# Five early groups instead of six, and later weights for them, in a kernel of banded attention, a low-rank mix, a channel layer and a gated layer

## The chip, the cores and the metric

One NeuronCore of a Trainium2 chip runs the whole program. The metric is the device time of one execution in microseconds (us). Engines: TensorE (PE in the rows, PEld its weight loads), VectorE (DVE), ScalarE (ACT), GpSimd (POOL) and SyncE (SP, which here only issues DMAs).

## What is computed

Four batches of 576 tokens. First comes attention with 8 heads of 64, scores limited to the 128 latest keys with a linear bias per head. Its output x (4 x 576 x 512) goes through the rest:

```
h = xt @ U @ V;  u = x + h.transpose(0, 2, 1)          # rank 32, over the tokens of a batch
y = u + np.maximum(u @ w_ch1, 0.0) @ w_ch2             # channel layer, 512 -> 2048 -> 512
h = np.maximum(y @ w_in, 0.0);  u, v = halves of h     # gated layer
out = (u * (w_spatial-mix of normalised v + b)) @ w_out
```

U, V and the weight matrices arrive as float64, so each of their words is put together on the chip from two 32-bit halves.

## The kernel before, in words

**How the order comes about.** The kernel does not write its instruction order by hand. It hands every step to a planner (`Plan`) as a task with an engine, a cost in the planner's own table, the buffers that it reads and writes, and a due number (`prio`). `Plan.run` goes through a simulated time: whenever an engine is free, it takes among the tasks whose inputs are there the one with the lowest due number. So a due number is no start time: a task with a high number still runs early where nothing else is ready, and it only steps back behind tasks with lower numbers that are ready at the same moment. DVE tasks marked `port` also wait until POOL is idle in the planner's time. The result is a fixed order on each engine, SP's queue of DMAs included, and on the chip each engine follows that order and waits where an input is late.

**Attention.** `heads(b, pair)` (L544) treats two heads of a batch at a time. The 16 pairs have due numbers p0 = 0, 20, 40, ..., 300 (10 per head; batch 0 has 0 to 60, batch 1 80 to 140). Within a pair the steps follow at p0 + 0 (loads of q and k, L553, L554), + 1 (scores on PE, L574), + 2 and + 3 (bias and row maximum on DVE, L582), + 3 and + 4 (exponentials on ACT, L587), + 4 (reciprocals of the sums, L597, L599), + 4 and + 5 (scaling of the probabilities on DVE, L607, or POOL, L605), then transposes (L614), the product with v (L628) and copies (L321 or L322). After two pairs `turned` transposes the output (L649); after four, `low_rank` (due 79 + 80 b, L665, L677, L682) adds the rank-32 mix, and the u of that batch is complete.

**Channel layer.** The 2048 hidden columns are cut into 16 blocks of 128, in four parts of 5, 4, 4 and 3 blocks (`parts`). Of part 0 there are ten weight tensors, called c = 0 to 9 here: c = 2f is the 512 x 128 piece of w_ch1 of block f, c = 2f + 1 the 128 x 512 piece of w_ch2. Each is loaded as 512 KB by one DMA (L354, due `early`), and converted (due `prio`): an absolute value on ACT (L360), a clip (L364 on POOL for c < 3, else L366 on DVE), and three DVE passes (L367, L370, L373) put the float32 together; then it is split exactly into two float32r halves, high (L383 on POOL for c < 5, else L321) and low (L388 on POOL). All DVE passes of it are `port` tasks.

Products are taken as three matmuls (high x high, low x high, high x low). `ffn_group` (L447) treats some tokens against the blocks of one part: it splits u into halves (L435, L438), multiplies with w_ch1 (L464 to L466), takes relu and the low half (L471 on ACT, L473 on DVE), multiplies with w_ch2 (L501 to L503), and adds into y (L511). It has two forms:
- early groups (`early=True`): `nb` groups of 256 tokens, part 0 alone, due 10000 + g on PE, so behind all attention work that is ready. They run between attention's matmuls. They have one buffer f1 for the first product (two blocks at a time) and one buffer acc for the second. Their evacuations have due number `evac` = 40. The split halves of u take four of the eight buffers of the ring x, so two groups are split at a time.
- late groups: 512 tokens at a time, from due 20000 on, with four buffers for the first product and four for the second. They need the pool that is opened when attention's buffers are given up, and four buffers of the ring x. Part 0 of the tokens that no early group took comes first, then parts 1, 2 and 3 of all tokens.

With `nb=6` early groups take tokens 0 to 1535, and part 0 of the other 768 is done by late groups of 512 and 256. One group of 256 tokens and part 0 has 120 matmuls (60 for each product).

The names and lines that matter:

```
part_of_hidden(0, r_wa, lambda c: 10 * (K["w0"] + K["w0s"] * c),     # L700 conversion due
                        lambda c: 10 * (K["d0"] + K["d0s"] * c), ...) # L701 load due
for g in range(NB):                                                   # L710
    ffn_group(g * 256, 256, parts_w[0], 1e4 + g, True, K["evac"], True)
t0 = NB * 256 if qi == 0 else 0                                       # L725
while t0 < NT:
    n = min(512, NT - t0)
```

V (L542) has due 40 for its conversion and 41 for its load.

Of the kernel before, what the change touches and what calls it, by code (L numbers as in the profile page):

```python
# [263 lines left out]
def tile_kernel(ctx, tc, qT, kT, v, U, V, w1, w2, w_in, wspT, bsp, w_out, bias, out):  # L264
# [32 lines left out]

    r_wa = Ring(in_left, "wa", max(12, 2 * K["parts"][0]))
    r_u = Ring(in_left, "u", 16)
    r_y = Ring(in_left, "y", 12)  # L300
    r_raw = Ring(in_left, "raw", 2)
    r_st = Ring(in_left, "st", K["nst"])
    r_h = Ring(in_left, "h", 8)
# [11 lines left out]

    PARTS = K["parts"]

# [10 lines left out]
    def engines(kind, usual):  # L328
        return BOTH if kind in K["flex"] else (usual,)

# [61 lines left out]
    def part_of_hidden(qi, ring, prio, early=lambda c: None, on_pool=lambda c: (False, False)):  # L392
        res = []
        for f in range(PARTS[qi]):
            c0 = (sum(PARTS[:qi]) + f) * 128
            two = []
            for i, args in enumerate(((block(w1, 0, E, c0, c0 + 128, 4), 4, 128), (block(w2, c0, c0 + 128, 0, E), 1, E))):
                c = 2 * f + i
                two.append(weights(ring, *args, prio(c), early(c), on_pool(c)))
            res.append(two)  # L400
        return res
# [137 lines left out]
    def low_rank_weights(prio, early, prio_v, early_v):  # L539
        single(u32, [(0, block(U, 0, 128, 0, RANK)), (1, block(U, 64, S, 0, RANK, 4))], 5, RANK, prio, None, early)  # L540
        P.add("DVE", 0.1, lambda: nc.vector.memset(u32[64:, 0], 0.0), w=[u32], prio=prio)
        single(v32, [(0, stacked(block(V, 0, RANK, 0, S), 4))], 1, S, prio_v, None, early_v)  # L542
# [143 lines left out]
    for h0 in range(0, H, 2):  # L686
        P.dma(128, 256, lambda h0=h0: nc.sync.dma_start(out=bias_t[:, h0 : h0 + 2], in_=bias[:, h0 : h0 + 2]),
              w=[bias_t.part(h0 // 2)], prio=10 * h0 + 0.5)
    low_rank_weights(15, 2, 10 * K["low"], 10 * K["lowd"])
    parts_w = [None] * 4  # L690
    for b in range(B):
# [7 lines left out]
        if b == 0:  # L699
            parts_w[0] = part_of_hidden(0, r_wa, lambda c: 10 * (K["w0"] + K["w0s"] * c),  # L700
                                        lambda c: 10 * (K["d0"] + K["d0s"] * c),  # L701
# [241 lines left out]

K = dict(parts=(5, 4, 4, 3), flex='xeht', cp=3, wp=5, low=4.0, w0=4.5, w0s=1.23, nb=6, evac=40.0, nst=3, d0=3.8, d0s=0.91, lowd=4.1)


# [38 lines left out]
```

## Time and profile before

| what | value |
|---|---|
| median of 3 runs | 805.63 us (803.71 to 806.95) |
| the profiled execution | 801.91 us, of it 800.1 us span from the first to the last instruction |
| PE busy | 767.1 us (96% of the span), 4852 matmuls |
| DVE, ACT, POOL busy | 430.7, 330.8, 278.0 us (54, 41, 35%) |
| chain that ended last | PE 84%, DVE 10%, DMA 3%, issue 1%, ACT 1% |

The chain that ended last is the work followed back from the last instruction, at each step to what released it. Busy shares are averages over stages with different limits: attention takes some 218 us of the span, the channel layer's late groups and the gated layer the rest. A matmul's duration in the rows is that of one pipelined instruction; what a matmul costs in a row of them is the distance between two starts.

### The profile page before, as it was taken

How to read it: one execution, taken by the hardware profiler on the slowest of the kernel's cores; microseconds unless marked ns; L12 is line 12 of the kernel's file. 1: busy time of each engine (PE TensorE's matmuls, PEld its weight loads, DVE VectorE, ACT ScalarE, POOL GpSimd, SP SyncE). 2: the span in 40 equal slices, each digit the busy share in tenths (PEclk: the TensorE clock that was granted, in tenths of full speed). 3: DMA queues.
4: the chain of work that ended last, by engine and by line, in shares of the span. 5: the costliest groups of instructions: out<-in, count | busy, mean ns of one | idle time of the engine just before them, and what ended most of it. 6: DMA issues, size and time to landing. Idle time of an engine off the chain costs nothing.

```text
span 800.1 us, 12918 instructions
## 1 busy us (share of the span) xinstructions
PE 767.1 (96%) x4852; PEld 654.4 (82%) x4852; DVE 430.7 (54%) x1128; ACT 330.8 (41%) x905; POOL 278.0 (35%) x354
## 2 busy tenths in 40 slices
PE   6779899999989999999999999999999999999998
PEld 4557777888888898888987889888998898898897
DVE  5789958678579367222487225832474415315220
ACT  6748848567453144121344214441343332332222
POOL 1545323120146146221376213762346114124021
PEclk9988999999999999999999999999999999999999
DMA  9842303210060052000320003000300000100101
GB/s 251 273 154 77 102 16 106 75 48 29 3 225 2 1 163 100 1 1 1 128 83 1 1 0 106 1 1 0 94 4 2 27 27 1 54 14 1 52 2 66
DMA packets 28834, 45.82 MB, mean 57 GB/s; under 512 B 4964, under 2 KB 18020, under 8 KB 28772
## 3 DMA queue, kind: packets, MB, share of 16 engines
q1 hardware_dynamic: 28772, 45.00, 17.6%
q8 instruction: 38, 0.62, 0.3%
q14 instruction: 24, 0.20, 0.1%
HBM read 40.27 MB, written 4.72 MB: 56 GB/s over the span
## 4 chain that ended last, share of the span: by engine, by line
PE 84%; DVE 10%; DMA 3%; issue 1%; ACT 1%; POOL 0%; SPq 0%; ACTq 0%; DVEq 0%; POOLq 0%
PE at L464 5%; PE at L465 5%; PE at L466 5%; PE sc L501 5%; PE sc L503 5%; PE sc L502 5%; PE at L614 3%; PE sc L574 3%; PE acc L501 3%; PE at L628 3%; PE acc L503 3%; PE f L464 3%; PE acc L502 3%; PE f L465 3%; PE f L466 3%; PE sc L769 2%
## 5 line engine op out<-in xcount | busy, mean ns | idle before, releaser
L438 POOL TENSOR_TENSOR x<-u,xc 128x192 fp32r<-128x192 f32 (+4 forms) x108 | 89.9, 865 | 136.2 <-ACT xc L435 133.4
L473 DVE SCALAR_TENSOR_TENSOR h<-at,h 128x512 fp32r<-128x512 f32 (+1 forms) x49 | 30.6, 624 | 115.5 <-ACT h L471 115.4
L471 ACT ACTIVATE h<-at 128x512 fp32r<-128x512 f32 (+1 forms) x49 | 26.7, 544 | 130.8 <-PE at L466 130.2
L587 ACT ACTIVATE p<-p,nmax 128x256 f32<-128x256 f32 (+2 forms) x160 | 72.8, 458 | 12.3 <-DVE nmax L582 11.9
L582 DVE CUSTOM_DVE_ANT_0 p<-sc,bias 128x256 f32<-128x256 f32 (+2 forms) x160 | 50.4, 362 | 17.0 <-PE sc L574 16.2
L614 PE MATMUL at<-ident,p 128*128 128x128 f32 x288 | 42.5, 288 | 13.5 <-DVE p L607 9.3
L574 PE MATMUL sc<-kr,qr 64*128 64x256 f32 (+2 forms) x320 | 43.9, 402 | 8.1 <-DMA kr<-in_kT 4.5
L388 POOL TENSOR_TENSOR wa<-st,wa 128x512 fp32r<-128x512 f32 x26 | 36.2, 1394 | 42.9 <-ACT wa L321 33.0
L614 PEld LDWEIGHTS at<-ident,p 128*128 128x128 f32 x288 | 33.2, 146 | 21.6 <-issue 6.9
L501 PE MATMUL acc<-h,wa 128*128 128x256 f32 (+1 forms) x150 | 47.5, 317 | 1.0 <-DVE y L511 0.9
L503 PE MATMUL acc<-h,wa 128*128 128x256 f32 (+1 forms) x150 | 45.0, 300 | 1.2 <-DVE h L473 1.1
L502 PE MATMUL acc<-h,wa 128*128 128x256 f32 (+1 forms) x150 | 44.6, 297 | 0.0
L466 PE MATMUL f<-x,wa 128*128 128x256 f32 (+1 forms) x148 | 44.4, 300 | 0.0
L574 PEld LDWEIGHTS sc<-kr,qr 64*128 64x128 f32 x320 | 29.9, 209 | 15.3 <-issue 6.7
L784 POOL TENSOR_TENSOR u<-y,u 128x576 fp32r<-128x576 f32 x16 | 23.0, 1456 | 54.8 <-ACT u L782 54.8
L471 ACT ACTIVATE h<-f 128x512 fp32r<-128x512 f32 (+1 forms) x34 | 18.0, 531 | 55.2 <-PE f L466 55.1
L464 PE MATMUL f<-x,wa 128*128 128x256 f32 x120 | 36.1, 300 | 4.6 <-DVE h L473 3.6
L607 DVE TENSOR_SCALAR p<-p,rinv 128x256 f32<-128x256 f32 (+2 forms) x128 | 39.7, 379 | 0.2
L503 PE MATMUL sc<-h,wb 128*128 128x512 f32 (+1 forms) x105 | 38.8, 370 | 0.0
L502 PE MATMUL sc<-h,wb 128*128 128x512 f32 (+1 forms) x105 | 38.8, 369 | 0.0
L501 PE MATMUL sc<-h,wb 128*128 128x512 f32 (+1 forms) x105 | 38.8, 369 | 0.0
L465 PE MATMUL at<-xc,wb 128*128 128x512 f32 (+1 forms) x104 | 38.5, 371 | 0.0
(329 smaller groups left out, 2347.9 us busy)
## 6 DMA issues: line engine op xcount, KB each, us to landing
wa<-in_w SPq DMA_DIRECT2D x18, 512.0 KB, 4.8
wb<-in_w SPq DMA_DIRECT2D x14, 512.0 KB, 5.5
qr<-in_qT SPq DMA_DIRECT2D x16, 288.0 KB, 4.0
kr<-in_kT SPq DMA_DIRECT2D x16, 288.0 KB, 3.5
vr<-in_v SPq DMA_DIRECT2D x16, 256.0 KB, 2.8
wa<-in_w_in SPq DMA_DIRECT2D x8, 512.0 KB, 4.4
out<-h SPq DMA_DIRECT2D x15, 256.0 KB, 2.0
wb<-in_w_out SPq DMA_DIRECT2D x4, 512.0 KB, 3.7
```

Source lines behind the costliest of these rows:

```text
L438: nc.gpsimd.tensor_tensor(out=tl[il][:, o : o + m], in0=ub[:, s : s + m], in1=f32(th[ih][:, o : o + m]), op=ALU.subtract)
L464: nc.tensor.matmul(o, wt[:, 0, k], a[ia], start=k == 0, stop=False)
L465: nc.tensor.matmul(o, wt[:, 1, k], a[ia], start=False, stop=False)
L466: nc.tensor.matmul(o, wt[:, 0, k], l[il], start=False, stop=k == 3)
L471: P.add("ACT", act(per * n), lambda f1=f1, hh=hh: nc.scalar.activation(out=hh.ap(), in_=f1.ap(), func=AF.Relu), r=[f1], w=[hh], prio=evac)
L501: nc.tensor.matmul(o, wt[:, 0, 0, c], hh[:, j], start=i == 0 and x == 0, stop=False, skip_group_check=True)
L502: nc.tensor.matmul(o, wt[:, 1, 0, c], hh[:, j], start=False, stop=False, skip_group_check=True)
L503: nc.tensor.matmul(o, wt[:, 0, 0, c], hl[:, j], start=False, stop=i == len(wts) - 1, skip_group_check=True)
L574: nc.tensor.matmul(s[j][:, c0 : c0 + n], qr[d, q0 : q0 + 128], kr[d, k0 : k0 + n], start=True, stop=True)
L582: nc.vector.tensor_tensor_reduce(out=p[:nq, c0 : c0 + nk], in0=s[:nq, c0 : c0 + nk], in1=bias_t[:nq, h, b0 : b0 + nk], scale=-0.125, scala ...
L587: nc.scalar.activation(out=p[:nq, c0 : c0 + nk], in_=p[:nq, c0 : c0 + nk], func=AF.Exp, scale=-1.0, bias=nmax[:nq, sl, t : t + 1], accum_o ...
L614: P.add("PE", 0.109, lambda pt=pt, c=c, p=pp[bk][j], c0=c0: nc.tensor.transpose(pt[:, c : c + 128], p[:, c0 : c0 + 128], ident), r=[pp[bk] ...
```

## The change

```
-K = dict(parts=(5, 4, 4, 3), flex='xeht', cp=3, wp=5, low=4.0, w0=4.5, w0s=1.23, nb=6, evac=40.0, nst=3, d0=3.8, d0s=0.91, lowd=4.1)
+K = dict(parts=(5, 4, 4, 3), flex='xeht', cp=3, wp=5, low=4.0, w0=6.5, w0s=1.23, nb=5, evac=40.0, nst=3, d0=5.5, d0s=0.91, lowd=4.1)
```

- `nb` 6 to 5: early groups take tokens 0 to 1279, and part 0 of the other 1024 is done by two late groups of 512.
- `w0` 4.5 to 6.5: the due numbers of the ten conversions go from 45, 57.3, 69.6, ..., 155.7 to 65, 77.3, 89.6, ..., 175.7, that is 20 more, the distance of two heads (one pair).
- `d0` 3.8 to 5.5: those of the ten loads go from 38, 47.1, ..., 119.9 to 55, 64.1, ..., 136.9.

The planner then makes a new order from these numbers on all engines and on SP.

## Rows read from the trace of the kernel before

**Rows 1.** Busy by stretch: PE, PEld, DVE, ACT, POOL (instructions), granted clock, DMA share, GB/s.

```profile
4.50:57.00 52.50, 40.74 (x324) 30.14 (x324) 40.68 (x152) 33.91 (x114) 20.78 (x25) 0.90 0.74 223
57.00:109.00 52.00, 45.62 (x382) 37.82 (x378) 47.47 (x170) 38.61 (x130) 22.59 (x31) 0.93 0.31 95
109.00:159.00 50.00, 48.37 (x470) 40.47 (x462) 35.91 (x151) 32.29 (x114) 10.61 (x22) 1.00 0.25 72
...
217.00:304.00 87.00, 81.95 (x557) 75.21 (x556) 57.26 (x103) 35.25 (x74) 40.25 (x40) 1.00 0.31 106
```

**Rows 2.** PE's instructions that read part 0's weights (wa), in batches 1 and 2.

```profile
57.00:109.00 52.00, 14.96 (x90) 0.93 0.31 95
109.00:159.00 50.00, 20.19 (x138) 1.00 0.25 72
```

**Rows 3.** Timeline of PE after attention: start, duration, [idle before, releaser].

```profile
229.34 0.38 PE L464 MATMUL f<-x,wa 128*128 128x256 f32 x1 [1.92 <-DVE h L473]
...
235.39 0.38 PE L464 MATMUL f<-x,wa 128*128 128x256 f32 x1 [1.48 <-DVE h L473]
...
241.60 0.36 PE L501 MATMUL acc<-h,wa 128*128 128x256 f32 x1 [0.92 <-DVE y L511]
...
245.27 0.28 PE L464 MATMUL f<-x,wa 128*128 128x256 f32 x1
...
259.19 0.39 PE L503 MATMUL acc<-h,wa 128*128 128x256 f32 x1 [0.73 <-DVE h L473]
```

**Rows 4.** Busy time in 20 us of late groups of 512.

```profile
320.00:340.00 20.00, 20.00 (x89) 16.40 (x88) 4.81 (x7) 2.82 (x7) 4.33 (x7) 1.00 0.00 1
```

**Rows 5.** Timeline of POOL after attention: splits of group 5, then the late group.

```profile
218.02 0.74 POOL L438 TENSOR_TENSOR x<-u,x 128x256 fp32r<-128x256 f32 x1 [34.98 <-PE at L677]
...
236.16 7.06 POOL L438 TENSOR_TENSOR x<-u,xc 128x192 fp32r<-128x192 f32 x8
```

**Rows 6.** Timeline of DVE in batch 0: pair 1's scaling, then around c = 0, 1.

```profile
21.81 2.53 DVE L607 TENSOR_SCALAR p<-p,rinv 128x64 f32<-128x64 f32 x10
...
39.53 0.76 DVE L367 TENSOR_SCALAR st<-st 128x512 uint32<-128x512 uint32 x2
...
41.41 1.29 DVE L373 SCALAR_TENSOR_TENSOR st<-wa,st 128x512 uint32<-128x512 uint32 x2
42.61 1.03 DVE L597 TENSOR_SCALAR rinv<-sums 128x10 f32<-128x10 f32 x1
...
43.93 5.12 DVE L607 TENSOR_SCALAR p<-p,rinv 128x64 f32<-128x64 f32 x10
```

**Rows 7.** Timeline of ACT: the last exponential of pair 3.

```profile
40.32 0.20 ACT L587 ACTIVATION_READ_ACCUMULATOR p<-p,nmax 128x1 f32 x1
```

**Rows 8.** Timeline of POOL: first and last of four splits of c = 0, 1.

```profile
42.17 1.44 POOL L383 TENSOR_TENSOR wa<-st,one 128x512 fp32r<-128x512 f32 x1 [4.64 <-DVE st L373]
...
46.03 1.42 POOL L388 TENSOR_TENSOR wa<-st,wa 128x512 fp32r<-128x512 f32 x1
```

**Rows 9.** Waits of PE, 40 to 62 us: in total, times, longest.

```profile
PE at L614 <- DVE p L607: 3.5, 2, 2.8
```

**Rows 10.** Waits of PE, 57 to 114 us.

```profile
PE at L614 <- DVE p L607: 3.1, 2, 2.1
```

**Rows 11.** Tile wa, 0 to 130 us: last DVE pass of the ten conversions, durations, first and last start.

```profile
L373 DVE SCALAR_TENSOR_TENSOR st<-wa,st x10: 678/684/925, 41.4 to 103.0; 128x512 uint32<-128x512 uint32 x10
```

**Rows 12.** Timeline of SP: the load of c = 0, then pair 2's q.

```profile
7.14 0.59 SPq L354 DMA_DIRECT2D wa<-in_w  x1
8.52 0.34 SPq L553 DMA_DIRECT2D qr<-in_qT  x1
```

**Rows 13.** Busy time and granted clock at the start of batch 1.

```profile
60.00:65.00 5.00, 3.78 (x18) 2.72 (x18) 5.00 (x23) 5.00 (x22) 5.00 (x7) 0.61 0.49 134
65.00:70.00 5.00, 5.00 (x31) 4.59 (x32) 4.93 (x19) 2.81 (x13) 2.43 (x4) 0.71 0.11 42
70.00:75.00 5.00, 4.92 (x38) 3.69 (x35) 5.00 (x19) 3.79 (x15) 0.60 (x1) 1.00 0.37 118
```

## The prediction

> **What bounds the kernel now.** I read busy time by stretch first, then the waits of PE in each stretch, then the timelines of the engines around those waits. The first view says where time can be won at all [rows 1]. In batch 0 (4.50 to 57 us) PE is busy 40.74 of 52.5 us, in batch 1 45.62 of 52, in batch 2 48.37 of 50, and from the end of attention to the end of part 0 (217 to 304 us) 81.95 of 87. So there are 11.8 + 6.4 + 1.6 + 5.05 us without a matmul, and the granted clock is 0.90 and 0.93 of full in the first two. Everything behind 304 us is late groups and the gated layer, which the change doesn't touch; it shifts as a whole. From batch 2 on PE is the bound, and a step taken off another engine gives nothing; before that DVE is the limit more often (47.47 of 52 us busy in batch 1).
>
> Early groups are what PE does between attention's matmuls: 90 matmuls' worth in batch 1, 138 in batch 2 [rows 2]. They are no extra work, only work in another place, so the sum has three kinds of terms: work that is cheaper in another form, idle time that goes, idle time that comes.
>
> **Six groups to five: the work.** Removed are one early group and the late group of 256; added is a second late group of 512. Matmuls of 256 columns start 0.12 us apart (30 from 241.60 to 245.27 us) [rows 3], so 2 x 120 of them take 28.8 us. Those of 512 columns come at 89 in 20 us, 0.225 us each [rows 4]; 120 take 27.0 us. That is 1.8 us less on PE, which is the path here. The splits, evacuations and additions into y are of the same tokens in fewer pieces; they are costed at nothing, since PE waits for them only at the places that follow.
>
> **Six groups to five: the waits.** The 5.05 us without a matmul after attention are four waits, 1.92, 1.48, 0.92 and 0.73 us [rows 3]. All are of one kind: an early group has one f1 and one acc buffer, DVE is 57 of 87 us busy with part 1's conversions besides [rows 1], and nothing else is ready for PE. The first two lie in group 4's first product, the third before its second half, the last in group 5. Why is nothing else ready? The late group's splits run on POOL from 236.16 us, while group 5's ran at 218.02 us [rows 5]: both want the four buffers of ring x that group 3 gives up, and group 5 has them. With five groups the late group gets them 18 us sooner, and PE can take its matmuls (four buffers for the first product) when group 4 waits. The last wait goes with group 5. Ends: nothing gained beyond 0.73, or all 5.05; I take 3.0, since the third wait is for y, on a DVE as busy as before, and the first comes only some 2 us after the late splits could be done.
>
> **Later weights: batch 0.** In the timeline of DVE, the three passes of c = 0 and of c = 1, six instructions, run from 39.53 to 42.61 us, ahead of pair 3's reciprocals, and those (1.03 us) ahead of pair 3's ten scalings, which take 5.12 us [rows 6]. Pair 3's last exponential had ended by 40.5 us [rows 7]. Due numbers decide here: 45 and 57.3 against 64 for the reciprocals. With 65 and 77.3 the conversions step behind. What is on the path is 42.61 - 40.5 = 2.1 us of conversion, and the slow scalings: ten took 2.53 us for pair 1 [rows 6], 2.6 us less; beside them POOL ran the four splits of c = 0 and 1 (42.17 to 47.45 us) [rows 8]. PE waited for these scalings twice, 3.5 us together [rows 9]. Ends: 0, where the planner finds another place for the same work that is as bad, and 2.1 + 2.6 = 4.7, with the stretched reciprocals 5.5. I take PE's own recorded wait, 3.5. Next in line is then the transposes' and copies' chain of pair 3 and batch 0's low-rank mix, late by their own length.
>
> **A rule on that.** The Trainium skill, SBUF — State Buffer, section Who interferes with whom, says that VectorE and GpSimd share a pair of ports under an exclusive lock, and whichever comes second blocks. By it the four splits only find other DVE instructions to block wherever they go, and the 2.6 us would be moved, not saved; the sum would be 1 to 2 us worse. The traces can't settle that, as the new neighbours aren't in them.
>
> **Later weights: SP's queue.** The load of c = 0 is issued at 7.14 us, ahead of pair 2's q at 8.52 us [rows 12]: due 38 against 40. With 55 it steps behind pair 2's loads, the third piece of the bias, V and pair 2's v; the other nine move one place or so each. 512 KB at the 223 GB/s of this stretch [rows 1] are 2.3 us by which these come sooner. No wait of PE is put down to them in the rows I read, so I take 0, with -2.3 as the other end; a loss is excluded before c = 1, whose last pass on DVE is itself 20 due later. No wait is added to SP, only order.
>
> **Later weights: batch 1.** The ten conversions end on DVE between 41.4 and 103.0 us [rows 11]. One pair of heads is about 52 / 4 = 13 us, so the last two or three land behind batch 1, in batch 2, where DVE is 35.91 of 50 us busy [rows 1] and has room. That relieves DVE at the end of batch 1, where PE waited twice for scalings, 3.1 us together [rows 10]. Against it, group 0 starts a pair later and has fewer matmuls to offer while batch 1 waits for DVE. It has 90 there now, 10.8 us at 0.12; one pair of the four later, up to half of it, 5.4 us, is displaced to where PE is full already, and is paid if batch 1 doesn't get shorter by as much. Ends -3.1 and +5.4; I take the middle, +1.
>
> **The sum.** -1.8 - 3.0 - 3.5 + 0 + 1.0 = -7.3 us. Against the profiled execution's own 801.91 us that is 794.6. That execution lies 3.7 us below the median of 805.63, and the forecast is for a median, so 805.63 - 7.3 = 798.3, say **798.5 us**.
>
> **Rivals.** A measurement of this kernel can tell about 0.5%, 4 us, from no change.
>
> First, **the conversions collide elsewhere**. A due number holds a task back only where another is ready; in the planner's time DVE may be free, and c = 0 and 1 land in an equally bad place. Then batch 0 and 1 give nothing in sum and the late group's splits, queued on POOL behind part 1's, come no sooner. For it: the order on each engine is fixed by costs that the chip doesn't keep (a third pass is planned alike for all, and took 678 to 925 ns [rows 11]). Against it: pair 3's reciprocals were ready and did lose by due number. What stays is 1.8 + 0.73: 805.63 - 2.5 = 803.1.
>
> Second, on the other side, **batch 1 is starved**. Place: PE from 57 to 75 us. At 60 to 65 and 65 to 70 us the clock is 0.61 and 0.71 of full, so mostly the lower level of 1.2 GHz, after a stretch in which PE stood waiting; at 70 it is back at 2.4 GHz [rows 13]. In between lie the first 24 matmuls of group 0, from 65.23 us. If these come a pair later, the slow stretch lasts as much longer: 3.78 x 0.39 + 5.00 x 0.29 = 2.9 us once more, beside the displaced 5.4. With the sure 2.5 off, that is +5.8: 811.4. It decides when batch 1 holds fewer than some 45 group-0 matmuls and still takes 52 us. For it: DVE is the fuller engine there. Against it: batch 0 ending sooner brings batch 1 forward, and three conversions leave it. The Trainium skill, TensorE: Matmul & The Clock Gate, section HAM oscillation — how this bites in real kernels, says that gaps in the matmuls put the engine back to half rate until it works densely again, which speaks against taking filler out of a stretch with gaps. By that rule the second rival's extra 2.9 us come; the trace agrees that the clock fell after waits.
>
> **How the numbers follow.** Forecast (faster by over 4 us) 0.58; first rival 0.27; second 0.15. The best ends of all terms together give -1.8 - 5.05 - 5.5 - 2.3 - 3.1 = -17.8, which won't meet at once; half of the way from the sum to it is -12.5, 793. To the other side the range takes in the first rival and half of the second, 808. So 791.5 to 808.
>
> **What would show it.** In the changed profile: c = 0's passes on DVE behind pair 3's scalings, and those ten near 2.5 us; batch 0 over by 54 us instead of 57; the last conversion at 108 to 120 us; after attention, the late group's splits by 230 us and at most one wait of PE over 1 us; part 0 over some 7 us sooner. I am wrong if batch 1 shows as much idle PE as before with fewer group-0 matmuls and a clock below full beyond 70 us, if the waits after attention stay near 5 us, or if what is won before 57 us is gone again by 109 us.

## The result and the profile after

The changed kernel takes 792.23 us (median of 4 runs, 788.29 to 793.14) against 804.67 us for the kernel before (4 runs beside it, 803.35 to 806.95): a ratio of 0.9833 [0.9805, 0.9861], 13.4 us less by the ratio. In a second measurement (five runs against nine of the kernel before) it was 790.39 us and 0.9817 [0.9785, 0.9848]. The forecast was 798.5 us, 7.1 less than the median then known: right in sign, but little more than half of the gain. The first measurement lies 0.7 us inside the stated range, the second 1.1 us outside it.

The profiled execution of the changed kernel took 791.57 us, with a span of 789.8. From here on the span is cut where the work itself has its marks: the first low-rank matmul of each batch (L665), which ends the batch's attention, and the last matmul of part 0. The five cuts and the rest, for the kernel before (columns as in [rows 1]):

```profile
0.00:53.94 53.94, 38.07 (x268) 28.30 (x268) 37.66 (x147) 33.19 (x112) 19.58 (x32) 0.91 0.73 221
53.94:108.62 54.68, 47.93 (x415) 39.33 (x415) 50.23 (x173) 40.83 (x135) 25.15 (x36) 0.94 0.34 102
108.62:158.70 50.08, 48.45 (x463) 40.55 (x462) 36.18 (x151) 32.29 (x114) 10.61 (x22) 1.00 0.25 72
158.70:212.65 53.95, 53.72 (x505) 45.65 (x504) 37.99 (x160) 32.01 (x117) 5.62 (x13) 1.00 0.09 29
212.65:303.74 91.09, 86.04 (x621) 78.54 (x620) 59.11 (x106) 36.11 (x76) 39.99 (x40) 1.00 0.30 101
303.74:800.00 496.26, 492.91 (x2587) 422.04 (x2585) 209.59 (x392) 156.39 (x352) 177.04 (x213) 1.00 0.08 28
```

And for the changed kernel:

```profile
0.00:49.41 49.41, 37.59 (x269) 28.55 (x269) 33.48 (x149) 32.00 (x111) 12.65 (x25) 0.93 0.74 216
49.41:104.20 54.79, 47.83 (x398) 37.56 (x397) 53.06 (x176) 39.14 (x128) 27.52 (x34) 0.91 0.40 122
104.20:156.84 52.64, 52.33 (x492) 44.28 (x492) 38.83 (x156) 32.21 (x116) 15.44 (x31) 1.00 0.24 70
156.84:209.60 52.76, 52.65 (x493) 44.62 (x492) 37.73 (x160) 32.03 (x117) 5.87 (x14) 1.00 0.10 30
209.60:295.18 85.58, 83.97 (x500) 72.03 (x500) 67.92 (x109) 36.85 (x72) 40.91 (x37) 1.00 0.33 109
295.18:789.80 494.62, 490.90 (x2586) 422.07 (x2584) 203.72 (x382) 154.56 (x349) 174.48 (x211) 1.00 0.09 28
```

The second column is the length of each cut in us. Batch 0 is 4.53 us shorter, batch 1 0.11 longer, batch 2 2.56 longer, batch 3 1.19 shorter, part 0 after attention 5.51 shorter, the rest 1.64 shorter: 10.3 us between these two executions. PE's instructions on part 0's weights number 72, 168 and 169 in batches 1 to 3, where the same cuts of the kernel before hold 90, 139 and 181: 409 against 410, so the head start at the end of attention is the same, only shifted by one batch.

The waits of PE after attention (209 to 296 us; line, what it waited for, total, times, longest), against the four of [rows 3]:

```profile
PE acc L501 <- ACT h L471: 1.2, 1, 1.2
PE acc L503 <- DVE h L473: 0.3, 1, 0.3
```

The late group's splits stand where the prediction put them: 20 us ahead of [rows 5], and 6.1 us behind the end of attention instead of 23.5 (timeline of POOL):

```profile
215.73 5.82 POOL L438 TENSOR_TENSOR x<-u,xc 128x448 fp32r<-128x448 f32 x8 [0.51 <-ACT xc L435]
```

In batch 0 the passes of c = 0 and 1 stand behind pair 3's scalings, as against [rows 6] (timeline of DVE):

```profile
42.77 2.85 DVE L607 TENSOR_SCALAR p<-p,rinv 128x64 f32<-128x64 f32 x10
45.55 0.75 DVE L367 TENSOR_SCALAR st<-st 128x512 uint32<-128x512 uint32 x2
46.22 1.28 DVE L370 SCALAR_TENSOR_TENSOR st<-wa,st 128x512 uint32<-128x512 uint32 x2
47.42 1.28 DVE L373 SCALAR_TENSOR_TENSOR st<-wa,st 128x512 uint32<-128x512 uint32 x2
```

The ten scalings take 2.85 us instead of 5.12. The splits of c = 0 and 1 on POOL have moved with the conversions: they run from 48.18 us on, beside the next weight's passes, which take 1.47 and 1.64 us where the same passes can take 0.68 (timeline of DVE):

```profile
50.01 1.47 DVE L370 SCALAR_TENSOR_TENSOR st<-wa,st 128x512 uint32<-128x512 uint32 x1
51.52 1.64 DVE L373 SCALAR_TENSOR_TENSOR st<-wa,st 128x512 uint32<-128x512 uint32 x1
```

Behind them stand the additions that complete u (L682), for which PE waits 1.1 us; in the kernel before it was 0.2, with one slow pass (1.64 us) there.

Something new is in the timeline of ACT:

```profile
23.55 0.72 ACT L360 ACTIVATE v<-raw 128x576 f32<-128x576 f32 x1 [5.65 <-DMA raw<-in_V]
```

ACT stands 5.65 us before it copies the low-rank factor V (3.21 us in the kernel before), and PE then waits 4.0 us for a copy that ACT makes behind it (3.0 us before).

In batch 1 the wait for scalings has nearly gone, and the wait for the conversions of part 0's weights has grown from 0.8 us to 3.4 (waits of PE, 49 to 105 us, against [rows 10]):

```profile
PE f L464 <- ACT wa L321: 2.0, 1, 2.0
PE f L465 <- POOL wa L388: 1.4, 1, 1.4
...
PE at L614 <- DVE p L607: 0.4, 1, 0.4
```

### The profile page after: what moved, and what is told of

Its sections match the earlier page's. It is cut to its first block, busy times and chain, and to the rows that moved or that the text cites. A ratio compares the mean times of both kernels' runs of the same rounds, so it can differ in the third digit from the quotient of the medians.

```text
span 789.8 us, 12642 instructions
## 1 busy us (share of the span) xinstructions
PE 765.3 (97%) x4732; PEld 649.1 (82%) x4732; DVE 434.7 (55%) x1129; ACT 326.8 (41%) x891; POOL 276.9 (35%) x349
## 4 chain that ended last, share of the span: by engine, by line
PE 85%; DVE 10%; DMA 2%; ACT 2%; issue 1%; POOL 0%; SPq 0%; ACTq 0%; DVEq 0%; POOLq 0%
PE at L464 5%; PE at L465 5%; PE at L466 5%; PE sc L502 5%; PE sc L501 5%; PE sc L503 5%; PE at L614 3%; PE at L628 3%; PE acc L501 3%; PE sc L574 3%; PE acc L503 3%; PE acc L502 3%; PE f L464 3%; PE sc L769 2%; PE f L465 2%; PE f L466 2%
## 5 line engine op out<-in xcount | busy, mean ns | idle before, releaser
L438 POOL TENSOR_TENSOR x<-u,xc 128x64 fp32r<-128x64 f32 (+5 forms) x108 | 91.0, 879 | 126.8 <-ACT xc L435 125.7
L574 PE MATMUL sc<-kr,qr 64*128 64x256 f32 (+2 forms) x320 | 47.0, 414 | 8.0 <-DMA kr<-in_kT 4.4
L574 PEld LDWEIGHTS sc<-kr,qr 64*128 64x128 f32 x320 | 31.9, 216 | 16.6 <-issue 6.5
L501 PE MATMUL acc<-h,wa 128*128 128x256 f32 (+1 forms) x130 | 42.1, 324 | 1.4 <-ACT h L471 1.2
L503 PE MATMUL acc<-h,wa 128*128 128x256 f32 (+1 forms) x130 | 39.8, 306 | 0.3 <-DVE h L473 0.3
L502 PE MATMUL acc<-h,wa 128*128 128x256 f32 (+1 forms) x130 | 39.5, 304 | 0.0
L466 PE MATMUL f<-x,wa 128*128 128x256 f32 (+1 forms) x128 | 38.7, 303 | 0.0
L435 ACT CAST xc<-u 128x64 fp32r<-128x64 f32 (+5 forms) x108 | 38.4, 435 | 0.5 <-PE at L677 0.5
L464 PE MATMUL at<-xc,wb 128*128 128x512 f32 (+1 forms) x104 | 38.4, 369 | 0.0
L465 PE MATMUL at<-xc,wb 128*128 128x512 f32 (+1 forms) x104 | 38.3, 369 | 0.0
```

The lines of the kernel that those rows point to most:

```text
L438: nc.gpsimd.tensor_tensor(out=tl[il][:, o : o + m], in0=ub[:, s : s + m], in1=f32(th[ih][:, o : o + m]), op=ALU.subtract)
L464: nc.tensor.matmul(o, wt[:, 0, k], a[ia], start=k == 0, stop=False)
L465: nc.tensor.matmul(o, wt[:, 1, k], a[ia], start=False, stop=False)
L466: nc.tensor.matmul(o, wt[:, 0, k], l[il], start=False, stop=k == 3)
L501: nc.tensor.matmul(o, wt[:, 0, 0, c], hh[:, j], start=i == 0 and x == 0, stop=False, skip_group_check=True)
L502: nc.tensor.matmul(o, wt[:, 1, 0, c], hh[:, j], start=False, stop=False, skip_group_check=True)
```

## The experiments

Three things had to be told apart: what each half of the change gives, where 1.6 us of the rest went in which nothing was edited, and why the runs gain more than two profiles side by side. The expectations of the first four call the terms of the prediction theory A.

**The two halves.** Five groups alone (of the dictionary K):

```diff
-nb=6
+nb=5
```

> Five early groups alone (nb=5), the weights as early as before. Theory A (the two halves of the change add up): 1.8 us less work on PE and some 3.4 us of waits after attention gone, so 5.2 us faster than before (ratio 0.9935), and in the profile at most 2 us of waits of PE between 215 us and the end of part 0. Rival B (the waits went because the later weights changed what is left after attention): only the 1.8 us of work, ratio 0.998, waits after attention still near 5 us.

Measured: 799.31 us (6 runs), 0.9922 [0.9899, 0.9945], that is 6.3 us less, where theory A had 5.2 and rival B 1.8. Part 0 after attention took 85.54 us, with 1.5 us of waits, and the rest 494.5, all as in the changed kernel: the waits go with the sixth group, and theory A holds for this half. But batch 0 ended at 56.26 us and batch 1 at 113.49, where the profile that I had worked from has 53.94 and 108.62 with the same order of work up to there. The weights alone:

```diff
-w0=4.5 d0=3.8
+w0=6.5 d0=5.5
```

> Later weights alone (w0=6.5, d0=5.5), six early groups. Theory A: batch 0 ends 4.6 us sooner as in the changed kernel, batch 1 holds fewer matmuls of group 0 and gives some 1.5 us back, the waits after attention stay near 5 us; 3 us faster in all, ratio 0.996. Rival B: the later weights also take the waits after attention away: 8 to 10 us faster, ratio 0.989.

Measured: 796.66 us, 0.9896 [0.9869, 0.9923], 8.4 us less. Batches 0 and 1 end at 50.23 and 102.50 us, and the rest takes 496.3. That is the size that rival B had, but not its way: part 0 after attention still takes 90.81 us, with 3.3 us of waits. The halves add up: 6.3 + 8.4 = 14.7, and the whole gives 13.4 to 14.7. So the five groups are near their term (1.8 + 3.0) and the later weights are far from theirs (2.5). That half was cut once more, into conversions (w0 = 6.5 alone) and loads (d0 = 5.5 alone):

> Only the conversions' due numbers 20 later (w0=6.5), loads as before. Theory A: c = 0 and 1 step behind pair 3's scalings, which is the whole gain of batch 0, so the same as later weights alone, ratio 0.996, batch 0's mix near 49.4 us. Rival C (it is the loads' place in SP's queue that brings batch 0 forward): batch 0's mix stays near 54 us, ratio 1.000.

> Only the loads' due numbers 17 later (d0=5.5), conversions' due numbers as before. Theory A: the conversions still go by 45 and 57.3 and, once their data are there, still come ahead of pair 3's scalings; batch 0's mix at 53 to 54 us, ratio 0.998 to 1.000. Rival C: pair 2's q, k and V come 2 us sooner and batch 0 with them, and c = 0 arrives too late to stand in pair 3's way: mix near 50 us, ratio 0.996.

Measured: conversions 800.41 us, 0.9931 [0.9907, 0.9955]; loads 800.0 us, 0.9933 [0.991, 0.9957]; against 5.6 and 5.4 us the two together give 8.4. Theory A fell here: it gave the gain to the conversions and nothing to the loads. Rival C, which gave it to the loads by way of batch 0, fell too. Batch 0 ended at 53.9 and 54.8 us, so neither alone has what both have there. With the conversions' due numbers alone, five of the six passes of c = 0 and 1 still run ahead of pair 3's scalings, and these stay slow (timeline of DVE):

```profile
41.91 0.76 DVE L367 TENSOR_SCALAR st<-st 128x512 uint32<-128x512 uint32 x2
...
44.58 4.23 DVE L607 TENSOR_SCALAR p<-p,rinv 128x64 f32<-128x64 f32 x10
```

But batch 1 ended at 108.2 and 106.9 in each, 5 to 7 us ahead of the run with five groups. The gain that I had not counted lies before the end of batch 1, and much of it doesn't depend on which of the two is moved. With either moved, the granted clock is 1.00 in every 5 us from 55 to 115 us; that this is the cause of the gain is not shown, since with both moved there are low stretches again.

**Was the first profile a typical one?** The kernel before, unchanged, profiled again:

> The kernel before, unchanged, for a second profiled execution. The one that the prediction was worked from took 801.9 us where the median of all runs is 805 to 806, and reached the end of batch 0's attention (the first low-rank matmul) at 53.9 and that of batch 1 at 108.6 us; the run with five groups alone, whose order is the same up to there, was at 56.3 and 113.5. Theory S (the first profile was an untypically early one in batches 0 and 1, and the later weights gain more against a typical one): 55 to 57 and 112 to 115 us here, with the same 496.2 to 496.4 us after part 0. Rival: 53.9 and 108.6 within 1 us again; then the run with five groups lost 5 us in the two batches for a reason of its own.

Measured: 803.58 us, batch 0 to 55.6, batch 1 to 110.3, where theory S had 112 to 115. That is between the two, and decides little by itself. But the four runs below have the order of the kernel before up to the end of attention too, so there are seven profiles of one order:

| profile | batch 0 ends | batch 1 ends | batch 1's length | batch 3 ends |
|---|---|---|---|---|
| before | 53.94 | 108.62 | 54.68 | 212.65 |
| before again | 55.61 | 110.32 | 54.71 | 214.38 |
| late buffers as after | 55.65 | 112.76 | 57.11 | 216.82 |
| x turned | 56.02 | 113.15 | 57.13 | 217.21 |
| both turned | 56.34 | 113.44 | 57.10 | 217.48 |
| five groups alone | 56.26 | 113.49 | 57.23 | 217.55 |
| h turned | 56.71 | 113.99 | 57.28 | 218.03 |
| *changed* | 49.41 | 104.20 | 54.79 | 209.60 |
| *changed again* | 49.87 | 105.36 | 55.49 | 210.79 |
| *weights alone* | 50.23 | 102.50 | 52.27 | 207.91 |

Batch 1 has two lengths, 54.7 us in two executions and 57.1 to 57.3 in five; the profile of the prediction was of the rarer kind, and the earliest of all. The times of the kernel before split in a like way: of eleven on one chip, four are 802.8 to 804.2 us and seven 805.9 to 808.1; of nine on another, four are 802.3 to 803.4 and five 805.3 to 807.9. So what theory S says holds for the kernel before, though its bounds for this run did not: the first profile was untypically early. What differs between the kinds? Busy time and granted clock in batch 1, first of the short kind (before again), then of the long one (h turned):

```profile
60.00:65.00 5.00, 3.36 (x22) 2.34 (x22) 5.00 (x25) 4.49 (x18) 4.04 (x6) 0.78 0.67 166
65.00:70.00 5.00, 5.00 (x26) 4.35 (x25) 5.00 (x18) 3.65 (x17) 2.95 (x4) 0.54 0.42 118
...
75.00:80.00 5.00, 5.00 (x50) 4.16 (x49) 5.00 (x28) 4.47 (x16) 2.46 (x3) 1.00 0.06 23
105.00:110.00 5.00, 4.64 (x45) 4.19 (x41) 1.72 (x4) 2.68 (x9) 2.33 (x5) 1.00 0.22 59
```

```profile
60.00:65.00 5.00, 3.15 (x26) 2.34 (x22) 5.00 (x22) 3.90 (x15) 3.43 (x5) 1.00 0.89 250
65.00:70.00 5.00, 4.32 (x35) 3.85 (x35) 5.00 (x16) 3.64 (x17) 3.96 (x5) 1.00 0.40 124
...
75.00:80.00 5.00, 5.00 (x31) 4.21 (x31) 4.83 (x24) 2.86 (x10) 1.44 (x3) 0.68 0.01 2
105.00:110.00 5.00, 4.83 (x34) 3.67 (x35) 2.57 (x7) 1.75 (x4) 0.20 (x1) 0.66 0.00 0
```

Read the clock, third from the end, beside DVE's busy time (columns as in [rows 1]). In the short kind PE falls toward its lower level of 1.2 GHz at 60 to 70 us, while DVE works without a pause (5.00 of 5). There it costs nothing: in the long kind PE has its full clock there, and then waits 1.4 us for DVE's scalings at 71 to 74 us, a wait that the short kind hasn't. The long kind's low stretches come at 75 to 80 and 105 to 110 us, where PE is what the others wait for. All five long ones show both, at 70 to 80 and at 100 to 110 us; neither short one does. DVE shows the cost: its work runs 1.0 us behind the short kind from 62 to 79 us, as at the end of batch 0, and then waits for PE twice (h turned):

```profile
79.89 0.23 DVE L582 CUSTOM_DVE_ANT_0 p<-sc,bias 128x64 f32<-128x64 f32 x1 [0.17 <-PE at L614]
...
81.43 0.49 DVE L322 COPY u<-at 128x320 f32<-128x320 f32 x1 [0.68 <-PE at L628]
```

At 82 us it is 2.0 behind, and by the end of batch 1, past the second low stretch, 3.7 (113.99 against 110.32). The second stretch begins in the same nine transposes, behind the same wait, first in the short kind, then in the long one (timeline of PE):

```profile
103.00 1.17 PE L614 MATMUL at<-ident,p 128*128 128x128 f32 x9 [1.02 <-DVE p L607]
105.17 1.84 PE L614 MATMUL at<-ident,p 128*128 128x128 f32 x9 [1.02 <-DVE p L607]
```

So equal waits of PE are followed by the full clock in one execution and by the lower one in another. That the low clock costs PE this time is read off the traces; what puts an execution into one kind or the other wasn't tried. Batch 0 spreads too, from 53.94 to 56.71 us: the seven are within 0.6 us of each other at 22 us, and the other six 1.3 to 2.1 us behind the first at 35 us. Why is not shown.

**The rest, with the same matmuls.** After part 0 the kernels with six groups took 496.2 to 496.4 us and those with five 494.5 to 494.6. No wait there is over 0.5 us; the matmuls themselves stand closer, up to 5.56 us for a block of 24 against 5.44 to 5.48. One early group fewer shifts the rings of the split input (x) and of the hidden layer (h). Both were turned to that place at the start of part 1, together and singly:

```diff
+        if qi == 1:
+            r_x.slots = r_x.slots[4:] + r_x.slots[:4]
+            r_h.slots = r_h.slots[2:] + r_h.slots[:2]
```

> The kernel before, six early groups, with the buffers of the split input (x) turned by four and those of the hidden layer (h) by two when part 1 of the hidden layer begins: from there on each operand lies in the buffer in which it lies with five groups. After the last matmul of part 0 the kernels with six groups took 496.2 to 496.4 us and those with five 494.5 to 494.6. Theory P (which buffers the operands lie in sets the spacing of the matmuls): the 24-matmul blocks of 512 columns in part 1 fall from 5.44 to 5.56 us to 5.44 to 5.48 us, and the rest after part 0 takes 494.4 to 495.0 us. Rival Q (it is the smaller last group of part 0, 256 columns against 512, with its ten more VectorE instructions beside the start of part 1): the blocks stay and the rest takes 496.2 or more.

> As the run with both rings turned, but the x buffers alone. If the first matmuls' moving operand is what counts, blocks of 5.44 to 5.48 us and 494.4 to 495.0 us after part 0; if h alone counts, no change (496.2 or more). Theory Q: no change.

> As the run with both rings turned, but the h buffers alone. If h counts, 494.4 to 495.0 us after part 0; if x alone counts, or theory Q, 496.2 or more. The pattern of the blocks in the kernel before repeats every two groups, as the x buffers do, while the h buffers repeat every group, which speaks for x.

Measured: with h turned the rest is 496.2 us, as before. With x turned, or both, it is 507.9 to 508.0: the turned buffers are the ones that the last group of part 0 had just used, and PE waited 5.0 us for the hidden layer at part 1's start. That stall was my own, but behind it the blocks are still 5.44 to 5.56 us (with x turned they start at 330.99, 336.45 and 342.01), and from part 2's first matmul to the end it takes 402.4 us, as in the kernel before (402.6). So theory P falls for both rings. What remained was the memory that is opened after attention. There a buffer gets its place when it is first used, and with five groups the first xc (split input of a late group) is used ahead of the first wb (weights of parts 1 and 3). In the kernel before, seven buffers were laid out in the changed kernel's order:

```diff
+            for tag, w in [('xc_0', 512), ('half_0', 32), ('wb_0', 1024), ('xc_1', 512), ('xc_2', 512), ('xc_3', 512), ('wb_1', 1024)]:
+                late_["pool"].tile([128, w], F32, tag=tag, name=tag.split("_")[0], bufs=1)
```

> The kernel before, order unchanged, with the buffers of the memory that is opened after attention (split input xc, weights wb of parts 1 and 3) put at the addresses that they have in the changed kernel (there the first xc lies ahead of the first wb; here the first wb ahead of the first xc). Turning x and h left the spacing of the matmuls as it was, so the buffers that remain are these. Theory P2 (the addresses of xc and wb set the spacing): the rest after part 0 takes 494.4 to 495.0 us instead of 496.2 to 496.4, the 24-matmul blocks of part 1 5.44 to 5.48 us. Rival: 496.2 or more; then the 1.8 us go with the order of the work and not with a place in memory.

Measured: the rest takes 494.39 us. No instruction was moved. The same three starts in the timeline of PE, first before, then with the late buffers moved (two lines further down in the code):

```profile
323.06 0.40 PE L464 MATMUL at<-xc,wb 128*128 128x512 f32 x1
328.62 0.40 PE L501 MATMUL acc<-h,wb 128*128 128x512 f32 x1
334.17 0.39 PE L464 MATMUL at<-xc,wb 128*128 128x512 f32 x1
```

```profile
327.03 0.39 PE L466 MATMUL at<-xc,wb 128*128 128x512 f32 x1
332.47 0.39 PE L503 MATMUL acc<-h,wb 128*128 128x512 f32 x1
337.91 0.39 PE L466 MATMUL at<-xc,wb 128*128 128x512 f32 x1
```

From one to the next are 24 matmuls: 5.56 and 5.55 us, then 5.44 and 5.44. Theory P2 holds: the 1.8 us in the rest are the place of these seven buffers in memory, of which the matmuls read xc and wb.

**Can more be had?** The changed kernel again, as the base, and then with V's load and copy three heads later, and with the weights later still:

> The changed kernel again, beside the kernel before on the same chip, for a second profile and as the base of the two runs below. Theory S (the changed kernel's first batches spread as those of the kernel before do, whose end of batch 1 lay between 108.6 and 114.0 us in six profiles of one order): 790 to 794 us, batch 0 ends at 48 to 51 us, batch 1 at 103 to 107.

```diff
-low=4.0 lowd=4.1
+low=7.0 lowd=7.1
```

> The changed kernel with the low-rank factor V loaded and copied three heads later too (low 7.0, lowd 7.1 instead of 4.0, 4.1). In the changed kernel ScalarE waits 5.65 us for V's load at 18 to 24 us, with a copy and three exponentials behind it, and TensorE then waits 4.0 us for a copy of ScalarE; V is first read at the end of batch 0. Theory T (that wait is what is left of batch 0's start): the wait is gone, batch 0 ends at 45.5 to 47.5 us instead of 49.4, and the time falls by 2 to 4 us. Rival U (the first conversion of part 0's weights, which now stands where V's copy stood on ScalarE, waits for its own load, with the queue of transfers as the bound): ScalarE waits 4 us or more there, no gain (within 1 us).

```diff
-low=4.0 lowd=4.1 w0=6.5 d0=5.5
+low=7.0 lowd=7.1 w0=7.5 d0=6.0
```

> As the run with V later, and part 0's weights converted one more head later and loaded half a head later (w0 7.5, d0 6.0), so that on ScalarE neither V's copy nor a conversion stands among the work of the first three pairs. Theory T: no ScalarE wait on a load over 1 us after 15 us but that of pair 3's own operands, batch 0 ends at 45 to 47 us. What batch 1 does is open: group 0 waits for the last conversions (it waited 3.4 us for them in the changed kernel), and each us that they come later is a us of idle TensorE there. Estimate 788 to 791 us; if batch 1 gives it all back, 792 to 794.

Measured: 790.39 us, 0.9817 [0.9785, 0.9848] for the changed kernel again, with batches 0 and 1 within theory S's bounds; 792.88 us, 0.9855 [0.9826, 0.9884] with V later; 792.86 us, 0.9843 [0.9817, 0.9868] with both later. Neither is better than the change as it stands; the intervals overlap, and both estimates of a gain were missed. In the profile with V later, ACT's wait is gone and batch 0 ends at 45.97 us, as theory T has it, but the next cuts read:

```profile
45.97:102.63 56.66, 47.92 (x385) 36.97 (x384) 52.33 (x172) 38.52 (x125) 25.43 (x35) 0.85 0.38 116
102.63:155.22 52.59, 52.17 (x493) 44.19 (x492) 40.10 (x155) 34.07 (x122) 18.54 (x33) 1.00 0.23 69
155.22:209.18 53.96, 53.73 (x506) 45.66 (x505) 37.99 (x160) 32.00 (x117) 5.77 (x14) 1.00 0.10 29
```

Batch 1 is 56.66 us long instead of 54.79, at a clock of 0.85, with PE waiting 4.5 us for scalings again, and batch 3 is 1.2 longer with its 12 matmuls more: of 3.4 us won, 0.4 are left at 209 us. With both later, batches 0 to 3 end at 199.01 us, 10.6 earlier, at full clock from 45 us on. But PE has then done 361 instructions on part 0's weights instead of 409, and part 0 after attention takes 92.97 us with 5.5 us of waits for h. The time lies in the 792 to 794 us that were expected if batch 1 gave all back, but batch 1 gave nothing back (48.94 us long instead of 54.79): the loss is after attention. Here an early end of attention was worth only what it still carried of part 0.

## Why the prediction was right and where it failed

*Five groups, the work and the waits* (1.8 + 3.0 = 4.8): right. Part 0 after attention is 5.51 us shorter, and the 5.05 us of [rows 3] have become 1.5. The reason holds too: the late splits start at 215.73 us, and PE takes the late group's matmuls from 224.21 us on, in the middle of group 4, where it had nothing. The third wait, which I thought would stay, went as well, and in its place one of 1.2 us on ACT.

*Later weights, batch 0* (3.5): right in size against the same profile (4.53) and in what it does there: c = 0 and 1 stepped behind pair 3's scalings, and these got fast again (2.85 us). But "Due numbers decide here" was wrong of the conversions alone: with w0 = 6.5 and the loads as before they didn't step behind, the scalings took 4.23 us, and batch 0 ended at 53.9. It took the loads as well. By the rule in the Trainium skill, SBUF — State Buffer, Who interferes with whom, the second of VectorE and GpSimd to ask for their shared ports blocks. The prediction took from it that the splits on POOL would block other DVE work instead, 1 to 2 us worse. The trace agrees in part: beside the splits, which now start at 48.18 us, the next weight's passes took 1.47 and 1.64 us, and PE's wait for the additions behind them grew from 0.2 to 1.1 us. Batch 1 as a whole is 0.11 us longer.

*SP's queue* (0): by the loads alone 5.4 us were to be had, and 2.8 beside the conversions (8.4 - 5.6), so 0 was wrong as a value for the runs. The profiles show it as an earlier end of batch 1, not as a wait of PE on a load; the two moves overlap, and how each makes its gain stays open.

*Later weights, batch 1* (+1): the sign was right for two profiles side by side. Batches 1 to 3 together are 1.48 us longer. DVE's scalings hold PE up for 0.4 us instead of 3.1, 18 instructions of group 0 are displaced into batch 2, and PE waits 3.4 us for the conversions instead of 0.8. One forecast of detail failed: the last conversion ends at 104 us and not at 108 to 120.

*The first rival* (conversions collide elsewhere, 803.1) didn't come for the whole change; its place was right with the conversions alone, its price was not (800.41). *The second* (batch 1 starved) is there in part: at 95 to 100 us both profiles of the changed kernel have a clock of 0.66, behind waits of PE. But group 0 kept 72 instructions, above the 45 from which it was to decide. The Trainium skill, TensorE: Matmul & The Clock Gate, HAM oscillation — how this bites in real kernels, says that gaps bring the half rate back. The trace agrees that low stretches come behind waits, but the same wait of 1.02 us is followed by full clock in one execution and by the lower one in another. What decided here is whether the low stretch falls where PE is awaited.

**The step that failed** is the last of the sum: "That execution lies 3.7 us below the median of 805.63, and the forecast is for a median, so 805.63 - 7.3". I took the 3.7 us for scatter that both kernels would have. They were a loss in batches 0 and 1 that most executions of the kernel before have and that its profiled one had not: batch 3 ends at 212.65 us there and at 216.8 to 218.0 in five of seven. The terms of the later weights, summed on that profile, gave 2.5 us, and between these two profiles 3.05 us came (212.65 to 209.60). Between typical executions, 217.5 (the middle one of the five) against 209.6 and 210.8, it is 6.7 to 7.9 us, and the runs gave 8.4. That term was mis-sized by some 5.9 us. Why the later weights take that loss away is not shown, only that they do. A second, smaller one is missing altogether: 1.8 us in the rest, which I had called untouched, because the change moves buffers in memory that the later matmuls read. That the first measurement lies inside the range is luck: half of the way to the best ends gives 793 in the prediction's own words, and 791.5 as the lower bound has no working.

## What to carry to other kernels

Before terms are added up on one profile, look where its time stands among the runs: an execution 4 us under the median may have left out something that the others pay, and a change may remove just that, so price it from a second profile. Work taken off an earlier stage may be worth only what the next bound stage still needs of it: two versions that ended attention's first batch 3.4 to 4.2 us sooner gained nothing. And a kernel whose buffers get their places by first use changes its memory with its order; compare the spacing of equal matmuls before explaining a small gain by the schedule.

## What the hardware did that I had not expected

One order of instructions has two lengths of batch 1, 54.7 and 57.2 us, by where TensorE's clock is low: at 60 to 70 us, under a busy DVE, it costs nothing, at 70 to 80 and 100 to 110 us it costs 2.5. The lower clock came behind a wait of 1.02 us in one execution and not behind the same wait in another. Matmuls of 512 columns stand 0.2267 us apart with xc and wb in one place and up to 0.2317 in another (5.56 / 24), with the clock at 1.00 in both: 1.8 us in all, 0.7 of it in part 1 (93.83 us from part 0's last matmul to part 2's first before, 93.16 with the seven buffers moved). Which of the seven buffers it is, and why, stays open.
